# A new order of the steps in the front and in the repeated row of a fused attention and expert kernel

## The chip, the core and the metric

The kernel runs on one core of a Trainium2 chip. A core has a matrix engine (TensorE, PE in the profile; its weight loads are shown as PEld), a vector engine (VectorE, DVE), a scalar engine (ScalarE, ACT), GpSimd (POOL) and SyncE (SP), which here issues the transfers. Each engine works through its own queue of instructions in order and waits on semaphores for the others. The metric is device time in microseconds (us) of one execution, lower is better.

## The reference

Gated linear attention over 4 batches, 8 heads, 768 positions and head size 48, followed by a layer of 8 experts on all 3072 tokens (width 384, hidden 1024), whose weights per token come from a softmax that is balanced by 8 rounds of Sinkhorn scaling.

```python
for t in range(S):
    state = alpha[:, :, t, :, None] * state + np.einsum('bhd,bhe->bhde', k[:, :, t], v[:, :, t])
    y[:, :, t] = np.einsum('bhd,bhde->bhe', q[:, :, t], state)
...
logits = x @ w_gate
P = np.exp(logits - logits.max())
for _ in range(8):
    P /= P.sum(1, keepdims=True) + 1e-09
    P /= P.sum(0, keepdims=True) + 1e-09
    P *= N / E
for e in range(E):
    h = np.maximum(x @ w1[e], 0.0)
    out += P[:, e:e + 1] * (h @ w2[e])
```

## The kernel before

The attention is done in chunks of 128 tokens, 24 in all, two to a unit (12 units of 256 tokens). A chunk turns k, q and the decays so that the head size lies on partitions, forms scores level by level (pairs of 1, 2, 4 ... 64 tokens, each level with the decays multiplied in), multiplies them with v, adds the part of the running state, and writes the result as two half-precision parts (high and low) into `xT`, the input of the experts. Chunks 0 to 3 do all levels directly in 13 steps (`direct_chunk`): step 2 turns the inputs, steps 3 to 9 are the levels, step 10 makes the output in psum (`psy`), step 11 its norm and the new state `ST`, step 12 `xT`, step 13 the gate's logits (`psg`). From chunk 4 on the lower levels come from blocks: a block (`attn_block`, 16 steps for a unit) multiplies q, k and products of them on POOL and DVE and reduces them on DVE (`tmp`, `AB`, `qt`, `al`), and sends the result through memory to the chunk, which then has 6 steps (`attn_chunk`).

The first three experts are computed with the attention still running. Their tiles are generators (`moe_tile`) which give out a "filler" at a time: in a tile's first half nine matmuls into a psum buffer `ps`, a Relu on ACT and the low half `h` on DVE, eight times; in its second half six matmuls of `ps` from `h` and `w2`, evacuated by ACT as `r`. Psum has four buffers for these. A tile is pushed when its tokens' `xT` and the expert's first weight are done. Each expert's weights are loaded, measured and split into two halves in 16 steps (`load_expert`).

What sets the order is one list of words: START up to chunk 7, then UNIT once for every later unit (eight times), with the numbers counted up. A word takes one step of something: `c2` a step of chunk 2, `b3` of block 3, `d2` the decays of a unit, `w1` a step of expert 1's weights, `g` one of the gate's weights, and `f` gives out 0.45 us worth of fillers, by a nominal price of a filler. A capital letter sets `lop` for that step: products that otherwise go to DVE are then put on POOL, or a weight's low half on POOL with an extra pass on ACT. `early_` holds back words whose inputs are not there. On every engine the instructions stand in the order of these words.

When the list is at its end, the rest of the fillers run with the Sinkhorn rounds; then the other five experts follow in a part of their own (`first`, `second`), whose order the list doesn't touch.

Of the kernel before, what the change touches and what calls it, by code (L numbers as in the profile page):

```python
# [25 lines left out]
def tile_gla_moe(ctx: ExitStack, tc: tile.TileContext, q, k, v, alpha, wg, w1, w2, out):  # L26
# [14 lines left out]
    UNIT = 'f f f f f f f f f f f f f f f f c1 f f c0 f B1 f f f f f f f f c1 f f f f f f f f b1 f f B1 f f b1 f f b1 f f b1 f f b1 f B1 f f f f f f c0 f f B2 f f f f f f f f c1 c0 f f B1 f f c1 f c1 f f f f f d1 f f c1 f f f f f f f f f c2 f f f b2 f f f f f f c2 f f f f f f f f f f b2 b2 B2 B2 b2 f c0'.split()
# [718 lines left out]
    w0, w1_, w2_ = (load_expert(e, wAB[e]) for e in range(NA))  # L760
# [84 lines left out]
    def later(a, g):  # L845

        if a[0] not in "bBcd":
            return a
        m = int(a[1:]) + (g * NCH if a[0] == "c" else g)
        return a[0] + str(m) if m < len(chunks if a[0] == "c" else units) else None  # L850


    order = START + [later(a, g) for g in range(NS // NCH, len(units)) for a in UNIT]
    order = [a for a in order if a]
# [308 lines left out]
```

## Time and profile before

| | us |
|---|---|
| median of 3 runs | 1732.25 (1730.5 to 1732.73) |
| profiled execution | 1735.68 |
| its span, first to last instruction | 1734.0 |
| PE busy | 1650.9 |
| DVE, ACT, POOL busy | 1221.1, 796.8, 290.9 |
| mean granted TensorE clock | 0.975 |

A row of the profile names the line, which here is mostly that of a helper (L58, L67, L70), so the tiles tell the steps apart. What stands in brackets in a timeline is the idle time of that engine ahead of the row and what ended it. The attention and the first three experts take the first 840 us or so, the other five experts the rest.

### The profile page before, as it was taken

To read this page: it belongs to the slowest core of one execution; us is meant where nothing else is said; L and a number is where in the kernel's file an instruction comes from. 1 tells how busy PE (TensorE), PEld (TensorE's weight loads), DVE (VectorE), ACT (ScalarE), POOL (GpSimd) and SP (SyncE) were. 2 spreads that over 40 slices of the span, in tenths; PEclk is the share of its full clock that TensorE was granted. 3 is DMA by queue.
4 is the path that set the end of the run, shared out by engine and by line. 5 is a ranking of instruction groups with operands and counts; after the bars stand their busy time and mean duration, and the time that the engine had idled before them with its cause. 6 is when DMAs were issued, how large, how long until landed. Compare 5 with 4: busy or idle time off the path is not lost.

```text
span 1734.0 us, 46403 instructions
## 1 busy us (share of the span) xinstructions
PE 1650.9 (95%) x19984; PEld 1420.5 (82%) x19984; DVE 1221.1 (70%) x2992; ACT 796.8 (46%) x1592; POOL 290.9 (17%) x262
## 2 busy tenths in 40 slices
PE   5679999999999999999999999999999999999999
PEld 4556767777777777776899999999999999999998
DVE  5767767666656766355577878888788867786666
ACT  3456433334333434334465545554555445544443
POOL 2424245435533633000000000000000000000000
PEclk7679999999999999999999999999999999999999
DMA  7153422442243133021202020202020201000001
GB/s 178 37 124 87 105 63 60 100 100 61 59 101 89 48 90 73 24 61 55 69 24 70 29 65 25 69 28 58 28 65 29 51 2 38 2 1 20 29 29 38
DMA packets 149501, 98.91 MB, mean 57 GB/s; under 512 B 108464, under 2 KB 139440, under 8 KB 149296
## 3 DMA queue, kind: packets, MB, share of 16 engines
q1 hardware_dynamic: 149296, 95.95, 21.2%
q8 instruction: 156, 2.56, 0.6%
q14 instruction: 49, 0.40, 0.1%
HBM read 67.63 MB, written 28.30 MB: 55 GB/s over the span
## 4 chain that ended last, share of the span: by engine, by line
PE 78%; DVE 15%; ACT 3%; issue 2%; POOL 1%; DMA 1%; SPq 0%; ACTq 0%; DVEq 0%; POOLq 0%
PE ps L67 49%; PE ps2x L67 12%; PE ps2v L67 3%; PE ps2z L67 3%; DVE h L58 3%; PE ps2y L67 3%; PE psy L67 2%; PE psl L67 2%; DVE hf L58 2%; DVE w L58 1%; ACT h L58 1%; DVE acc L58 1%; DVE decq L58 1%; DVE AB L58 1%; DVE deck L58 1%
## 5 line engine op out<-in xcount | busy, mean ns | idle before, releaser
L67 PE MATMUL ps<-xT,w 128*128 128x256 f16 (+1 forms) x6984 | 806.9, 273 | 16.2 <-DVE h L58 11.5
L67 PEld LDWEIGHTS <-w 128*128 128x128 f16 x6984 | 676.5, 98 | 99.4 <-issue 18.4
L67 PEld LDWEIGHTS <-h 128*128 128x128 f16 x6768 | 588.0, 98 | 118.4 <-issue 9.4
L58 ACT CAST h<-hf 128x896 f16<-128x896 f32 x240 | 224.8, 937 | 337.6 <-DVE hf L58 227.6
L58 DVE TENSOR_TENSOR h<-hf,h 128x896 f16<-128x896 f32 x240 | 261.5, 1089 | 165.5 <-ACT h L58 164.0
L67 PE MATMUL ps<-w,h 128*128 128x384 f16 x1728 | 297.1, 327 | 0.5 <-DVE h L58 0.4
L67 PE MATMUL ps2x<-w,h 128*128 128x192 f16 x2880 | 267.7, 246 | 7.6 <-DVE ps2z L58 5.5
L58 DVE TENSOR_TENSOR hf<-hf 128x128 f32<-128x128 f32 x960 | 235.3, 286 | 39.5 <-ACT hf L58 30.8
L58 DVE SCALAR_TENSOR_TENSOR h<-ps,h 128x256 f16<-128x256 f32 (+1 forms) x296 | 115.6, 411 | 140.9 <-ACT h L58 140.3
L58 ACT ACTIVATE h<-ps 128x256 f16<-128x256 f32 (+1 forms) x296 | 110.3, 377 | 164.1 <-PE ps L67 164.1
L58 ACT ACTIVATE hf<-ps 128x512 f32<-128x512 f32 x240 | 142.4, 593 | 54.1 <-PE ps L67 54.1
L58 POOL TENSOR_TENSOR tmp<-qt,kt 128x768 f32<-128x768 f32 (+1 forms) x80 | 133.2, 1670 | 126.9 <-DVE qt L58 72.7
L58 ACT COPY r<-ps 128x384 f32<-128x384 f32 x72 | 34.4, 479 | 158.5 <-PE ps L67 144.1
L58 DVE TENSOR_REDUCE AB<-tmp 128x16 f32<-128x768 f32 (+2 forms) x90 | 80.7, 903 | 33.5 <-POOL tmp L58 33.3
L67 PE MATMUL ps2v<-w,h 128*128 128x192 f16 x720 | 70.2, 248 | 0.0
L58 ACT COPY A<-psl 16x128 f32<-16x128 f32 (+3 forms) x164 | 52.5, 327 | 37.5 <-PE psl L67 25.3
L67 PE MATMUL ps2y<-w,h 128*128 128x192 f16 x720 | 69.2, 246 | 0.0
L67 PE MATMUL ps2z<-w,h 128*128 128x192 f16 x720 | 69.2, 246 | 0.0
L58 DVE SCALAR_TENSOR_TENSOR acc<-ps2x,pe,acc 128x192 f32<-128x192 f32 x120 | 49.2, 410 | 1.8 <-PE ps2x L67 1.8
L67 PE MATMUL psl<-T 48*32 48x16 f32 (+2 forms) x1472 | 24.1, 219 | 27.4 <-DVE T L58 10.9
L67 PEld LDWEIGHTS psl<-T 48*32 48x32 f32 (+1 forms) x1472 | 20.7, 139 | 31.8 <-DVE T L58 12.4
L58 ACT ACTIVATE w<-w2f,s_w 128x768 f16<-128x768 f32 x35 | 32.6, 933 | 30.5 <-DVE w2f L58 29.1
(186 smaller groups left out, 1325.5 us busy)
## 6 DMA issues: line engine op xcount, KB each, us to landing
raw<-r SPq DMA_DIRECT2D x72, 192.0 KB, 1.9
ri<-raw SPq DMA_DIRECT2D x72, 192.0 KB, 2.4
w1f<-in_moe_w_dram SPq DMA_DIRECT2D x20, 384.0 KB, 7.0
w2f<-in_moe_w_dram SPq DMA_DIRECT2D x5, 1536.0 KB, 7.0
VN<-in_v_dram SPq DMA_DIRECT2D x48, 96.0 KB, 3.0
xT<-in_moe_w_dram SPq DMA_DIRECT2D x6, 768.0 KB, 4.6
out_dram<-acc SPq DMA_DIRECT2D x24, 192.0 KB, 2.0
qt<-in_q_dram SPq DMA_DIRECT2D x10, 384.0 KB, 4.7
```

The source lines that it names most:

```text
L58: r = f(*a, **k_)
L67: tc.keep_in_program_order(nc.tensor.matmul(out_, lhsT, rhs, start=start, stop=stop, **k_))
```

## The change

START and UNIT are replaced by other lists, which were searched for anew with half the TensorE clock assumed at the front. START has 1972 words (1996 before), 1783 of them f (1807); UNIT 131 (132), 102 of them f (103). The other words are the same steps, in other places and with other capitals. The heads of both lists, cut:

```diff
-    START = 'c0 C0 f c0 f c0 c1 f c0 f C1 f f c0 f f f ...'.split()
-    UNIT = 'f f f f f f f f f f f f f f f f c1 f f c0 f B1 f f f f f f f f c1 f f f f f f f f b1 f f B1 f f b1 f f b1 f f b1 f f b1 f B1 f f f f f f c0 f f B2 f f f f f f f f c1 c0 f f B1 f f c1 f c1 f f f f f d1 f f c1 f f f f f f f f f c2 f f f b2 f f f f f f c2 f f f f f f f f f f b2 b2 B2 B2 b2 f c0'.split()
+    START = 'c0 C0 C0 C0 f C1 f c0 f f f f f f f f C1 f f ...'.split()
+    UNIT = 'f f f f f f f f f f f f f f c1 f f c0 f f f f f f f B1 f f f f f b1 f f f f f f f B1 f f f f b1 B1 f f b1 f f B1 b1 f f b1 f f f f f c0 f c1 f f f f f f B2 c1 f f f f f f c0 f f c1 f f f f f d1 f f f f c1 c2 f f f f f f f f c1 f f f f c2 c0 f f f f f f f f b2 f f f f f B2 f b2 f B2 f B2 b2'.split()
```

Where it moves instructions, at three places. First, VectorE at the end of chunk 3 (the names end in batch and chunk, 0_3; `w11` is the low half of expert 1's first weight, `h1_0_256` that of the next tile's h). Before:

```order
L58 TENSOR_TENSOR T_0_3_1249<-T_0_3_1249,D64_0_3_1876 128x2x4x64
L58 SCALAR_TENSOR_TENSOR w11_1_826<-xT0_1_80,s_w1_1_1816,w10_1_825 128x768 x2
L58 TENSOR_SCALAR m_0_3_2010<-psy_0_3_1969 128x128
L58 TENSOR_SCALAR st_0_3_2012<-m_0_3_2010 128x128
L58 TENSOR_TENSOR ys_0_3_2014<-psy_0_3_1969,st_0_3_2012 128x384
L58 TENSOR_SCALAR pw_0_3_2016<-m_0_3_2010 1x128
L58 TENSOR_TENSOR ST0_119<-ST0_119,pss_0_3_2018 48x4x48 x2
L58 SCALAR_TENSOR_TENSOR w11_1_826<-xT1_1_83,s_w1_1_1816,w10_1_825 128x768
L58 TENSOR_TENSOR xT1_0_82<-ys_0_3_2014,xT0_0_79 128x3x128
L58 SCALAR_TENSOR_TENSOR h1_0_256_2036<-ps1_0_256_0_2037,h0_0_256_2035 128x256
```

Now, in the same place:

```order
L58 TENSOR_SCALAR m_0_3_2010<-psy_0_3_1969 128x128
L58 TENSOR_SCALAR st_0_3_2012<-m_0_3_2010 128x128
L58 TENSOR_TENSOR ys_0_3_2014<-psy_0_3_1969,st_0_3_2012 128x384
L58 TENSOR_SCALAR pw_0_3_2016<-m_0_3_2010 1x128
L58 TENSOR_TENSOR ST0_119<-ST0_119,pss_0_3_2018 48x4x48 x2
L58 TENSOR_TENSOR xT1_0_82<-ys_0_3_2014,xT0_0_79 128x3x128
L58 SCALAR_TENSOR_TENSOR w11_1_849<-xT1_1_83,s_w1_1_1740,w10_1_848 128x768
L58 SCALAR_TENSOR_TENSOR h1_0_256_2036<-ps1_0_256_0_2037,h0_0_256_2035 128x256
```

The last split of the weight has moved behind the low half of xT, and the two ahead of chunk 3's norm have left VectorE.

Second, VectorE around block 4's long product (`tmp8_1_1`, of batch 1, unit 1) and the first h's of the tile of tokens 512 to 767 (`h1_0_512`). Before:

```order
L58 TENSOR_REDUCE AB0_123<-tmp4_1_1_22_3378 128x4x4
L58 TENSOR_REDUCE AB0_123<-tmp4_1_1_23_3400 128x4x4
L58 TENSOR_TENSOR qt_1_1_3218<-qt_1_1_3218,al_1_1_3220 128x2x192
L58 TENSOR_TENSOR al_1_1_3220<-al_1_1_3220 128x2x48
L58 TENSOR_TENSOR tmp8_1_1_24_3443<-qt_1_1_3218,kt_1_1_3219 128x1536
L58 SCALAR_TENSOR_TENSOR h1_0_512_3446<-ps1_0_512_0_3447,h0_0_512_3445 128x256
L58 SCALAR_TENSOR_TENSOR h1_0_512_3446<-ps1_0_512_1_3459,h0_0_512_3445 128x256
L58 TENSOR_REDUCE AB0_123<-tmp8_1_1_24_3443 128x4x8
L58 SCALAR_TENSOR_TENSOR h1_0_512_3446<-ps1_0_512_2_3537,h0_0_512_3445 128x256
```

Now:

```order
L58 TENSOR_REDUCE AB0_123<-tmp4_1_1_22_3419 128x4x4
L58 SCALAR_TENSOR_TENSOR h1_0_512_3440<-ps1_0_512_0_3441,h0_0_512_3439 128x256
L58 SCALAR_TENSOR_TENSOR h1_0_512_3440<-ps1_0_512_1_3453,h0_0_512_3439 128x256
L58 TENSOR_REDUCE AB0_123<-tmp4_1_1_23_3428 128x4x4
L58 TENSOR_TENSOR qt_1_1_3181<-qt_1_1_3181,al_1_1_3183 128x2x192
L58 TENSOR_TENSOR al_1_1_3183<-al_1_1_3183 128x2x48
L58 TENSOR_TENSOR tmp8_1_1_24_3469<-qt_1_1_3181,kt_1_1_3182 128x1536
L58 SCALAR_TENSOR_TENSOR h1_0_512_3440<-ps1_0_512_2_3471,h0_0_512_3439 128x256
L58 TENSOR_REDUCE AB0_123<-tmp8_1_1_24_3469 128x4x8
```

Two h's have moved ahead of the block's long step. At the block before it (block 3, tile of expert 1) it is six instead of none.

Third, VectorE in a repeated row, at the end of a block (batch 2, unit 0) and the start of the next tile (`h1_0_1024`). Before:

```order
L58 TENSOR_TENSOR tmp8_2_0_42_5362<-qt_2_0_4712,kt_2_0_4713 128x1536
L58 TENSOR_REDUCE AB0_123<-tmp8_2_0_42_5362 128x4x8
L58 TENSOR_REDUCE AB0_123<-tmp4_2_0_43_5381 128x2x8
L58 TENSOR_REDUCE AB0_123<-tmp4_2_0_44_5396 128x2x8
L58 SCALAR_TENSOR_TENSOR h1_0_1024_5409<-ps1_0_1024_0_5410,h0_0_1024_5408 128x256
L58 TENSOR_TENSOR qt_2_0_4712<-qt_2_0_4712,al_2_0_4714 128x384
L58 TENSOR_TENSOR al_2_0_4714<-al_2_0_4714 128x48
L58 SCALAR_TENSOR_TENSOR h1_0_1024_5409<-ps1_0_1024_1_5425,h0_0_1024_5408 128x256
```

Now:

```order
L58 TENSOR_TENSOR tmp8_2_0_42_5285<-qt_2_0_4653,kt_2_0_4654 128x1536
L58 TENSOR_REDUCE AB0_123<-tmp8_2_0_42_5285 128x4x8
L58 TENSOR_REDUCE AB0_123<-tmp4_2_0_43_5322 128x2x8
L58 TENSOR_REDUCE AB0_123<-tmp4_2_0_44_5331 128x2x8
L58 TENSOR_TENSOR qt_2_0_4653<-qt_2_0_4653,al_2_0_4655 128x384
L58 TENSOR_TENSOR al_2_0_4655<-al_2_0_4655 128x48
L58 SCALAR_TENSOR_TENSOR h1_0_1024_5347<-ps1_0_1024_0_5348,h0_0_1024_5346 128x256
L58 SCALAR_TENSOR_TENSOR h1_0_1024_5347<-ps1_0_1024_1_5380,h0_0_1024_5346 128x256
```

The first h of the next tile has moved behind the block's last two products.

In the front, beside this: chunk 1's first level (step 3) goes ahead of chunk 0's step 8; chunk 3's step 9 ahead of the gate's third; block 2's steps 5 to 8 come earlier (5 and 6 ahead of the first tile, 7 and 8 among its first half), step 9 ahead of chunk 3's step 2; and its loads ahead of chunk 2's on SP's queue. Further on, chunk 7's step 1 comes behind chunk 6's step 5, and the logits of chunk 5 later. At the end the last chunk's logits come eight fillers ahead of the list's end.

More of the change, by code (lines that the diff above doesn't have):

```diff
@@ L41, in tile_gla_moe @@
[L41 removed]
+    START = 'c0 C0 C0 C0 f C1 f c0 f f f f f f f f C1 f f f f f f f f f f f f f f f f f f f f f f f f f C0 f f f f f f f f f f f w0 f f f f f f f f f f f c0 f f f f f f f f f f f f f f f f f f f f f f f f f f f f f f f f f f f f f f f f f f f f f f f f f f f f f f f f f f f f f f f f f f f f f f f f f f f f f f f f f f f f f f f f f f f f f f f f f f B2 f f f f f f f f f f f C1 f f f f f f f f C2 f f f f f f f f f f f f W0 w0 f f f f f f f f c0 c1 f f f f f f f f f w0 f f W0 f f f f f f f f f f f f C2 f f f f f f f f f f f f C1 f f f f w0 f f f f f f f f f f f f f f f f f f f f f f f f f f f f f f c0 f f f w0 f f f f f f f f f f f f f f f f f f C1 f f f f f f f f f f f f w0 f f f f f f f f f f f f f f f f f f f f f f W1 f f f f f f f f f f f f f f f f f f f f f f f f f f f f f f f f f f f f f f f f f f f f f f f f f f f f f f f f f f f C0 f f f f f f f f f f f f f f f f f f f f f f f f f f f f f f f f f f f f f f f f f f f f f f f f f f f f f f f f f f f f f f f f f f f f W1 C1 f f f f f f f f f f f f f f f f f f f f f f f f f f f f f f f f f f f f f f f f f f f f f f f f b2 f f f f f f f f f f f C0 f f f f f f f f f f f f f f f f f f f f f f f f w0 f f f f f f f f f f f f f f f f f f f f f f f f f f f f f f f f f f c1 f f f f f f f f f d2 f f f f f f f f f f f f f f f f f f f f f f f f f f f f f f f f f f f f f f f f f f f f f f f f f f f f f f c2 f f f f f f f B3 f f f f f f f f f f f f f B2 C1 f f f f f f f W0 f C3 f f f f f f f f f f f f f f f f f f f f f f f f f f f C1 f f f f f f f f f f f f f f f f f B2 c1 f f f f f f f f f f f f f f f f f f f f f g f f f f f f f f f f f f f f f f f f B2 f b2 f f c2 f f f f f f f f c0 f f b2 f f b2 f f f f c2 f f f f f f f f f f f f f f f f f c1 f f f w0 f f f f f f f f f f f f f f f f f f f f f f b2 f f f f f f f C3 f f f f f c2 f f f f f f f f f f f f f f f f f f f f f f f f f f f f f f f f W1 C3 f f f f f f f f f f f f f f f f f f f f f f f f f f f f f f f f f f c2 f f c2 f f f f f f f f f f f f f f f f f f f f f f w0 f f f f f f B3 f f f f f f f f f f f f f f f C3 f f f f f f f f f c0 f f f f f f f f f f f f f f c2 f f f f f f f f f f f f f f f f W0 f f f f f f f f f f f W1 f c3 f f f f f f f f w2 f f f f c2 b2 f f f f f f f f f f f f f f f f f f f f f f f f f f f f f f c2 f f f w0 f f f f w0 f f f f f f f f f f f f f f f f f f f f f f f c3 f f b2 f f f f f f g f f f f f f f f f f f f f W0 f f f f f f f f f f f f W1 f f f f C3 f f f f f f f f f f f f f f f f f f f f f f f f f f f f f f f f f f f f f f f f f f f f f f f f f f f f f f f f f f f f f f f f f C2 f f f B2 f f C3 f f f f f f f f b2 f f f f f B3 f w2 f f f f f f f w0 f f f f f w2 f f f f f f f f f f f f b3 f f f f f f f f w2 f f f B3 B2 f f f f f f f f f f f f f f f f f f f f f f f f f f f f f f f f f f f f f f f f f f f f f f f f f f B2 f f f f f f f f f f f f c3 f f C1 f f f g f f f f f f f W1 f d3 f f f f f f f f f f f f f f f f f f W1 f f f f c3 f f f f f f f f f f f f f f c3 f f f f f f f f f C3 w1 f f c4 f f f B3 f f f f W1 f f f f w1 f f f f f f B2 f f f f f f f f f f W1 f f f f f W1 f f f f f f f c4 f w2 f b3 f f f f f f f f f f f f f f f C2 f f w1 f f f f f f f W1 f f f f f f f f f f f f f f f f f f f f f f f f f f f f f f f f f f f f f f f f f f f f f f f f f f f f f f f f f f f f f f f f f f f f f f f f f f f f f f f f f f f f w2 f f f f f f f f f f f w2 f f f f c4 f f f f f f f f f f f f f c4 f w1 f f f f f f f f f f f w2 f f f f f f f f f f f f f f f f f f f f f f f f f f f f f f f f f f f f f f f f f f f f f f f f f f w2 f f f f f c4 f f f f f f f f f f f f f f f f f f w2 f f f f f f f f f w1 f f f f f C3 f f f f f f f f f f f b3 f f f f f f f f f f f f b3 f f f f B3 f f B3 B4 f B3 f f c4 f f c6 f b3 f f f f w2 b3 f f f B3 f f f f f f f f f f f f c5 f f f c5 w2 f f w2 c5 f w2 c5 w2 f f f f f f f f f f f f c5 f f f f w2 f f f f f f b3 f f f b4 f f f f f f f f f f f f f f b4 f w1 b4 f f f f f f f f f f f f c8 B4 f f f f c5 f f B4 f f f b4 f f b4 f f f f f f f f b4 f b4 f B4 c6 f b4 f f f f f B4 f c6 f f B4 f f B4 c6 f f f B4 f f c6 f f f f f c7 c6 f f B5 f c7 f f f f d4 f f f f f f f c7 f f c7 f f f f f f f f f c7 f f c7 c8 b5 B5 f f f f b5 B5 b5 b5 f'.split()
```

1 line of the change is left out of this document (removed).

## The prediction

> **What bounds the kernel now.** I read the page's totals first, then its slices, the busy times by stretch, TensorE's waits, and last the timelines around the longest of them.
>
> ```profile
> PE 1650.9 (95%) x19984; PEld 1420.5 (82%) x19984; DVE 1221.1 (70%) x2992; ACT 796.8 (46%) x1592; POOL 290.9 (17%) x262
> PE   5679999999999999999999999999999999999999
> PEclk7679999999999999999999999999999999999999
> PE 78%; DVE 15%; ACT 3%; issue 2%; POOL 1%; DMA 1%; SPq 0%; ACTq 0%; DVEq 0%; POOLq 0%
> ```
>
> TensorE is the bound: busy 1650.9 of 1734.0 us, and the chain lies on it for 78%. The 83 us in which it stands are mostly in the first three slices of 43 us, where its clock is low too. By stretch (start:end, length, busy time of PE, PEld, DVE, ACT, POOL, granted clock, DMA share, GB/s):
>
> ```profile
> 20.00:45.00 25.00, 12.75 (x478) 10.10 (x478) 11.86 (x33) 10.71 (x25) 2.54 (x5) 0.56 0.75 191
> 65.00:85.00 20.00, 8.62 (x433) 7.55 (x431) 18.13 (x41) 5.11 (x13) 10.65 (x9) 0.73 0.01 3
> sum 127.00, PE 77.74 PEld 62.42 DVE 81.99 ACT 55.42 POOL 41.38; mean PE 12.96 PEld 10.40 DVE 13.66 ACT 9.24 POOL 6.90
> sum 194.00, PE 181.54 PEld 137.11 DVE 137.56 ACT 90.29 POOL 80.58; mean PE 36.31 PEld 27.42 DVE 27.51 ACT 18.06 POOL 16.12
> 320.00:740.00 420.00, 415.84 (x5386) 318.09 (x5385) 260.14 (x502) 158.81 (x428) 168.94 (x129) 1.00 0.29 71
> 740.00:845.00 105.00, 97.75 (x750) 73.90 (x748) 57.60 (x156) 42.24 (x87) 0.00 (x0) 0.98 0.27 72
> ```
>
> The first sum is 0 to 127 us, the direct chunks 0 to 3: 49 us without TensorE. The second is 126 to 320: 12.5 us. The repeated row (320 to 740) loses 4.2 us, the change of phase behind it 7.2, and the order there is untouched. So the edit can win in a front where no engine is full and chunks go back and forth between PE and DVE, and in single waits up to 320; in the repeated row it can mostly lose.
>
> **The change part by part.** Every step is still taken once. Only places move, and by a step's capital letter some multiplications go from DVE to POOL or back. An "f" ahead of the first pushed tile emits nothing, so the f's at START's head are no time. TensorE's work and SP's transfers are the same in sum.
>
> *End of chunk 3.* The next tile's matmuls wait for chunk 3's low half of xT.
>
> ```profile
> 124.00 0.72 DVE L58 TENSOR_TENSOR ST<-ST,pss 48x192 f32<-48x192 f32 x2
> 124.76 1.02 DVE L58 SCALAR_TENSOR_TENSOR w<-xT,s_w,w 128x768 f16<-128x768 f32 x1
> 125.69 0.55 DVE L58 TENSOR_TENSOR xT<-ys,xT 128x384 f16<-128x384 f32 x1
> 126.30 4.00 PE L67 MATMUL ps<-xT,w 128*128 128x256 f16 x18 [1.48 <-DVE xT L58]
> ```
>
> A weight split of 1.02 us stands between ST and xT; it now stands behind xT: -1.0 (between -1.5, all of the wait, and 0). The two splits of that weight ahead of it go to POOL, with two passes on ACT instead of one; that is beside chunk 3's psy, so 0.
>
> *Gate weights.* Chunk 3's last level (16 small matmuls) moves ahead of the gate's.
>
> ```profile
> 112.41 0.84 ACT L58 COPY A<-psl 32x128 f32<-32x128 f32 x4
> 113.64 0.62 PE L67 MATMUL psg<-wg,xT 128*128 128x8 f16 x9 [2.60 <-ACT wg L58]
> 116.41 1.12 PE L67 MATMUL psl<-T 48*64 48x64 f32 x16
> 118.55 1.51 PE L67 MATMUL psy<-T,ST 128*32 128x128 f32 x24 [1.01 <-DVE T L58]
> ```
>
> The level still waits for ACT's copies out of psl (to 113.25), so most of the 2.60 stays; but DVE's T behind it then lies beside the gate's matmuls, and the 1.01 goes: -1.0 (-2.6 to 0).
>
> *First levels of chunks 0 and 1, first tile.* Chunk 1's scores now go ahead of chunk 0's sixth step, into TensorE's waits of 1.20 and 0.37.
>
> ```profile
> 23.36 0.60 PE L67 MATMUL psl<-T 48*32 48x32 f32 x28 [1.20 <-DVE A L58]
> 25.07 1.02 PE L67 MATMUL psl<-T 48*32 48x16 f32 x64 [0.37 <-DVE A L58]
> 29.78 0.43 PE L67 MATMUL psl<-T 48*32 48x16 f32 x28 [2.17 <-issue]
> 37.72 0.69 PE L67 MATMUL psl<-T 48*32 48x16 f32 x46 [3.81 <-issue]
> 30.00:35.00 5.00, 3.01 (x127) 2.55 (x113) 3.40 (x15) 1.56 (x4) 0.62 (x1) 0.50 1.06 243
> ```
>
> Behind them TensorE stands 2.17 and 3.81 us for nothing but its own issue, while the DMA engines are full (1.06). The same weights are loaded by then (b2's q, alpha and k only go ahead of chunk 2's loads on SP's queue, which chunk 2 first needs at 42 us), so whoever comes earlier waits longer: I take 0 of the 1.57. The Trainium skill's page "Runtime: NRT & Kernel Launch" (Instruction fetch mechanics) has the cost of crossing a block of code as mostly hidden; by it the 1.57 would be kept. This trace disagrees, if these stalls are the code's.
>
> Then b2's steps come sooner: two of them go in among the first tile's eight h's, and chunk 3's first T goes behind the long DVE step of b2.
>
> ```profile
> 72.06 0.69 DVE L58 TENSOR_TENSOR T<-psQR,D 128x512 f32<-128x512 f32 x1 [0.16 <-ACT QR L58]
> 78.07 0.94 DVE L58 TENSOR_REDUCE AB<-tmp 128x16 f32<-128x768 f32 x1
> 81.36 0.55 DVE L58 TENSOR_TENSOR xT<-ys,xT 128x384 f16<-128x384 f32 x1
> 82.86 0.84 PE L67 MATMUL psl<-T 48*32 48x16 f32 x64 [3.78 <-DVE T L58]
> ```
>
> The long step takes 78.07 to 81.4 and TensorE stands 3.78 us behind it now. In the new order chunk 3's T stands behind it: it would come at about 78.9 instead of 72.06, some 6.8 us later, while the b2 work is over sooner. DVE has the same rows ahead of the second tile either way (the sum of their mean durations is 82.8 us in both orders). I take 0, with -1.6 and +6.8 as ends. Front: -2.0.
>
> *From 126 to 275 us.* Four waits lose their cause.
>
> ```profile
> 181.68 2.13 PE L67 MATMUL ps<-xT,w 128*128 128x256 f16 x18 [1.80 <-DVE h L58]
> 204.68 0.20 PE L67 MATMUL psg<-wg,xT 128*128 128x8 f16 x2 [1.07 <-ACT xT L58]
> 205.45 0.33 PE L67 MATMUL psg<-wg,xT 128*128 128x8 f16 x7 [0.56 <-DVE xT L58]
> 240.29 2.13 PE L67 MATMUL ps<-xT,w 128*128 128x256 f16 x18 [1.70 <-DVE h L58]
> 246.82 0.66 PE L70 MATMUL psq<-ident,QN 128*128 128x128 f32 x4 [0.68 <-ACT Tk L58]
> 174.65 1.75 DVE L58 TENSOR_TENSOR tmp<-qt,kt 128x1536 f32<-128x1536 f32 x1
> 236.53 3.37 DVE L58 TENSOR_TENSOR tmp<-qt,kt 128x1536 f32<-128x1536 f32 x1
> ```
>
> The 1.80 and 1.70 have one cause: a block's long product (tmp, 1.75 to 3.37 us) stands on DVE ahead of the tile's first h's, and TensorE runs out of psum buffers. In the new order six h's stand ahead of it in the first place, and two in the second. From the first I take -1.3, as the last two h's still wait (0 to -1.8); from the second -1.7 (0 to -1.9). Of the psg waits 1.63 go, since fillers lie between xT and psg now, but chunk 5's psy and its norm follow each other without a filler, for about the 0.6 us from ACT's ab: -1.0 (-1.6 to +0.6). Chunk 7's transposes come after chunk 6 has given its psum buffer back: -0.7. Sum -4.7.
>
> *Repeated row.* Each row has had a wait of about 0.5 us for DVE's decq:
>
> ```profile
> PE psl L67 <- DVE decq L58: 2.5, 5, 0.5
> 307.14 3.11 PE L67 MATMUL ps<-xT,w 128*128 128x256 f16 x27 [1.39 <-DVE h L58]
> 753.53 0.27 PE L70 MATMUL pst_gg<-ident,gm 128*1 128x128 f32 x1 [0.96 <-DVE gm L58]
> ```
>
> Five fillers lie now between a chunk's transposes and its scores instead of four: at most -2.5; I take -1.0. At the end the last logits come eight fillers before the phase ends, so gm is ready when TensorE gets to it: -1.0 (-1.3 to +1).
>
> *Waits that the new order makes.* The old trace can't show them. The sum so far removes 8.7 us of waits that I could see; an order with the same work must have some of its own (126 to 320 has 12.5 us now, of which I listed 5.8). I give 40% back, +3.5; ends 0 and +11.
>
> Sum: -2.0 - 4.7 - 1.0 - 1.0 + 3.5 = -5.2. The profiled execution took 1735.68 us (span 1734.0 and 1.7 around it), so 1730.5; the median shown, 1732.25, is 3.4 below that execution, which gives 1727.1.
>
> **The rivals.**
>
> *Nothing is given back.* Without the +3.5 it is 1723.6, and with the 1.57 us of the first levels 1722.0. For it: the placed waits each have one cause that is gone. Against it: the 3.81 us of issue.
>
> *No change.* The 6.8 us of chunk 3's T decide the front: its six levels follow one another, each a PE block of about 0.85 and a T of 0.69. Then -5.2 + 6.8 = +1.6, 1733.9. For it: the wait of 3.78 us shows such a chain. Against it: from 65 to 85 us DVE is busy 18.13 of 20, so what b2 no longer needs later comes back.
>
> *Slower, by the repeated row.* In the new row a block's last reduces, qt and al all stand on DVE ahead of the first h of the next tile; before, that h stood ahead of qt and al. The 1.39 us above at 307 is such a wait, in the one place where the old order had it so. If every one of the eight rows has it, it is 8 x 1.39 = 11.1 on top of the other terms without the row's -1.0: +6.9, 1739.2. It turns slower by over 0.2% (3.5 us) from 1.0 us per row, (3.5 + 4.2) / 8. Against it: seven or eight second-half fillers of about 0.96 us, which need nothing of DVE, now lie over the block's rows.
>
> *A better clock in the front.* Between 20 and 45 us TensorE's 12.75 us run at a granted clock of 0.56. If shorter gaps kept the clock full there, they would take 12.75 x 0.56 = 7.1; with half of the 5.6 us saved on the path, since DVE is about as busy, it is 2.8 less: 1724.3. For it: waits of 1.20 and 0.37 are filled. Against it: the 2.17 and 3.81 stay. The Trainium skill's "TensorE: Matmul & The Clock Gate" (Part 1) speaks for it: an idle window of about 3.4 us halves the clock and a busy one restores it; here the low clock outlasts windows in which TensorE was busy half the time, so the trace neither bears it out nor excludes it.
>
> **How the numbers follow.** A run of this kernel differs from no change visibly at about 0.2%, 3.5 us. Forecast, 1727.1 (1724.5 to 1728.7): 0.44. Nothing given back, 1722 to 1724: 0.10. A better clock, 1724: 0.04. No change, 1728.8 to 1735.7: 0.25. Slower: 0.17. So faster 0.58, same 0.25, slower 0.17. The range leaves about 2 in 10 out: its low end is 2 below the rival without new waits, its high end lies short of the full repeated row. The forecast's own range is 1723 to 1730.
>
> **What would show it.** Right: the w split behind chunk 3's xT and the first 256-wide matmul at about 124 instead of 126.3; no wait over 1 us for h near 180 and 240, none for psg near 205; TensorE busy over 183 us between 126 and 320; gm's wait gone. The issue stalls near 28 and 34 stay and end at about the same times. Wrong: chunk 3's xT after 127; a wait of 1 us or more for h in each repeated row; or new waits between 126 and 275 of more than 5 us in all.

## The result, and the profile after

| | before | after |
|---|---|---|
| median, us | 1732.25 (1730.5 to 1734.55) | 1721.51 (1719.51 to 1725.42) |
| ratio | 1 | 0.9939 (95%: 0.9927 to 0.995) |
| profiled execution, its span, us | 1735.68, 1734.0 | 1721.51, 1719.8 |
| PE, DVE, POOL busy, us | 1650.9, 1221.1, 290.9 | 1645.5, 1203.7, 283.4 |

Faster by 10.7 us (8.7 to 12.6). The forecast was 5.2 us faster, 1727.1, with a range of 1720 to 1737 that takes in the rivals: the sign and that range held, the size is twice what was said, and the forecast's own range, 1723 to 1730, was missed by 1.5 us. The page of the changed kernel, its totals and the clock row of its slices:

```profile
PE 1645.5 (96%) x19984; PEld 1419.6 (83%) x19984; DVE 1203.7 (70%) x2993; ACT 793.1 (46%) x1592; POOL 283.4 (16%) x261
...
PEclk9789999999999999999999999999999999999999
```

Two things changed: TensorE stands less (74.3 us instead of 83.0), and it is busy 5.4 us less with the same matmuls. Both are found by stretch. First of before, then of the changed kernel; the stretches end at 130 us, at 262 us, at the largest logit (gm) and at the end; the columns are length, PE busy, granted clock, DMA share, GB/s.

```profile
0.00:130.00 130.00, 80.74 (x2308) 0.73 0.47 113
130.00:262.00 132.00, 121.65 (x1479) 0.98 0.34 86
262.00:753.50 491.50, 484.60 (x6303) 1.00 0.29 71
753.50:1734.00 980.50, 963.96 (x9899) 1.00 0.13 39
```

```profile
0.00:130.00 130.00, 87.36 (x2350) 0.87 0.50 120
130.00:262.00 132.00, 123.95 (x1569) 1.00 0.36 90
262.00:738.80 476.80, 469.88 (x6148) 1.00 0.30 73
738.80:1719.80 981.00, 964.31 (x9923) 1.00 0.13 37
```

The two spans differ by 14.2 us, the medians by 10.7: the execution of before that was profiled is 3.4 us above its median, so its front is not to be taken as typical (see "All of them in one account"). Idle time is length less busy time. It falls by 6.6 us in the front (49.3 to 42.6) and 2.3 in the next stretch (10.3 to 8.0). In the repeated row it is 6.9 in both, at the end 16.5 and 16.7. The rest is clock. In before the clock behind 130 us is at half to 132.2 us, and then for single periods of 3.41 us, beginning at 166.4, 511.1, 801.3 and 845.6 us; in the changed kernel there is none. Two of the four, each with the period ahead of it, in before (busy times of PE, PEld, DVE, ACT, POOL, then the clock):

```profile
507.70:511.10 3.40, 1.74 (x84) 1.38 (x84) 2.74 (x6) 0.77 (x2) 1.06 (x1) 1.00 0.00 0
511.10:514.50 3.40, 3.40 (x67) 2.69 (x57) 0.95 (x2) 1.66 (x5) 1.60 (x1) 0.50 0.02 5
797.80:801.30 3.50, 0.83 (x8) 0.75 (x8) 0.76 (x2) 3.44 (x9) 0.00 (x0) 0.99 0.00 0
801.30:804.70 3.40, 3.40 (x18) 2.42 (x17) 1.51 (x4) 1.92 (x6) 0.00 (x0) 0.51 0.00 0
```

Ahead of each of the four stands a period in which TensorE stood for about half of the time or more (busy shares 0.47, 0.51, 0.23 and 0.42). TensorE is busy all through the halved one, and loses half of it, 1.7 us: the 256-column matmuls in the period at 801.3 us start 0.213 us apart, those at full clock 0.109. The waits ahead of it are ordinary ones (TensorE's timeline; in brackets the wait):

```profile
509.43 1.14 PE L67 MATMUL ps<-xT,w 128*128 128x256 f16 x9 [1.66 <-DVE h L58]
...
800.47 4.77 PE L67 MATMUL ps<-xT,w 128*128 128x256 f16 x27 [2.76 <-DVE h L58]
```

In the changed kernel the wait of 2.76 has become two, 1.46 and 1.39 us, and an edge of a period (787.7) falls between them:

```profile
784.30:787.70 3.40, 1.94 (x17) 1.49 (x16) 0.00 (x0) 3.33 (x8) 0.00 (x0) 1.00 0.08 29
787.70:791.10 3.40, 2.01 (x19) 1.75 (x18) 1.77 (x5) 2.15 (x7) 0.00 (x0) 1.00 0.10 34
791.10:794.50 3.40, 3.40 (x30) 2.69 (x29) 1.94 (x9) 1.85 (x4) 0.00 (x0) 1.00 0.00 0
```

Nearly the same idle time, parted by an edge, leaves the clock alone here. Over the fourteen profiles of this study, behind 130 us, each of the 21 periods in which TensorE was busy for a share of 0.43 or less was followed by one at half clock, none with 0.62 or more was. In between both occur: of 17 periods from 0.43 to 0.52 six were followed by one at half clock, of 52 from 0.52 to 0.62 two were. "Clock loss" below is half of TensorE's busy time in such periods: 7.8 us behind 130 us in before, 0 in the changed kernel.

### The profile page after: what moved, and what is told of

Its sections match the earlier page's. It is cut to its first block, busy times and chain, and to the rows that moved or that the text cites. A ratio compares the mean times of both kernels' runs of the same rounds, so it can differ in the third digit from the quotient of the medians.

```text
span 1719.8 us, 46369 instructions
## 1 busy us (share of the span) xinstructions
PE 1645.5 (96%) x19984; PEld 1419.6 (83%) x19984; DVE 1203.7 (70%) x2993; ACT 793.1 (46%) x1592; POOL 283.4 (16%) x261
## 4 chain that ended last, share of the span: by engine, by line
PE 74%; DVE 17%; ACT 4%; issue 2%; POOL 2%; DMA 1%; ACTq 0%; SPq 0%; POOLq 0%; DVEq 0%
PE ps L67 46%; PE ps2x L67 12%; DVE h L58 4%; PE ps2z L67 3%; PE ps2v L67 3%; PE ps2y L67 3%; DVE hf L58 2%; PE psy L67 2%; DVE AB L58 2%; PE psl L67 2%; POOL tmp L58 2%; DVE tmp L58 2%; ACT h L58 2%; DVE w L58 2%; ACT w L58 1%
## 5 line engine op out<-in xcount | busy, mean ns | idle before, releaser
L67 PE MATMUL ps<-xT,w 128*128 128x256 f16 (+1 forms) x6984 | 806.9, 273 | 10.3 <-DVE h L58 4.0
L67 PEld LDWEIGHTS <-w 128*128 128x128 f16 x6984 | 676.0, 98 | 90.8 <-issue 12.6
L67 PE MATMUL ps<-w,h 128*128 128x384 f16 x1728 | 293.4, 326 | 3.7 <-DVE w L58 1.9
L58 POOL TENSOR_TENSOR tmp<-qt,kt 128x768 f32<-128x768 f32 (+1 forms) x80 | 125.2, 1569 | 161.0 <-DVE AB L58 86.9
L58 ACT COPY r<-ps 128x384 f32<-128x384 f32 x72 | 34.3, 478 | 195.4 <-PE ps L67 150.9
L58 ACT COPY A<-psl 16x128 f32<-16x128 f32 (+3 forms) x164 | 52.5, 327 | 36.5 <-PE psl L67 26.8
L58 DVE SCALAR_TENSOR_TENSOR acc<-ps2x,pe,acc 128x192 f32<-128x192 f32 x120 | 49.3, 411 | 1.8 <-PE ps2x L67 1.8
L58 ACT ACTIVATE w<-w2f,s_w 128x768 f16<-128x768 f32 x35 | 32.4, 933 | 27.3 <-DVE w2f L58 27.3
```

Of the source, the lines that this page charges most:

```text
L58: r = f(*a, **k_)
L67: tc.keep_in_program_order(nc.tensor.matmul(out_, lhsT, rhs, start=start, stop=stop, **k_))
```

## The experiments

The expectations speak of a theory of the clock at first (the new head keeps the clock full from 23 us on, and that is the gain), then of a theory of the grid (the periods of 3.41 us, as above, behind 130 us). The theory of the waits is the forecast's own. In the diffs f11 stands for eleven words f. Each ratio is to before, with its 95% interval.

### The new front alone (e1_front)

```diff
-    order = START(new) + UNIT(new) x 8
+    order = START(new) up to chunk 3's step 12 + all steps left over in the order of before
```

> The changed kernel's steps up to chunk 3's transposed input (xT), then the steps of the kernel before in their old order (the steps it had already done ahead of that point left out). Theory of the clock and of the fetch stall (the new head fills TensorE's throttle period up to 23.0 us, the granted clock stays full to about 60 us, and chunk 3's xT comes 4.5 us earlier, all of which is kept): about 1727.8 us against 1732.25, ratio 0.9974, and no period at half clock begins at 23.0 us. Theory of the waits (the front is worth what the forecast gave it, the weight split and the gate weights, 2.0 us): 1730.2 us, ratio 0.9988. Third possibility (what is early at chunk 3 only waits later, since the old middle is bound by VectorE): 1732, ratio 1.000.

Measured 1730.62 us, ratio 0.9992 (0.9984 to 1.0001): -1.5 us. Nothing like the 4.5 us by which chunk 3's xT comes earlier in the traces is kept. The value is near the forecast's front (-2.0), and 0 is inside its interval; that it is the front's waits is not shown, since this profile also has fewer periods at half clock further on than before (two, 3.2 us). The half clock began at 23.0 us here as in before.

### The new order to chunk 7, the old row (e2_rowold)

```diff
-    UNIT = (new)
+    UNIT = (before)
```

> The changed kernel's order up to chunk 7 with the repeated row of before. Theory from the two traces (the lead is made ahead of 310 us, about 9.8 us, and the new row is worth about nothing but the 0.96 us wait for the largest logit at the end, its new waits taking back what the removed ones gave): 1722 to 1723 us, ratio 0.9945 to 0.995 against before. Theory of the forecast (the new row gains 2.0 for waits removed and loses 3.5 in new ones): 1720.0 us, ratio 0.993. Third possibility (the row is worth the 3 to 4 us by which the lead grows between 310 us and the end): 1724.5 to 1726, ratio 0.9955 to 0.9965.

Measured 1728.45 us, 0.9978 (0.9968 to 0.9988): -3.7 us, beyond the slow end of all three. All three were wrong: the row is worth some 6.9 us once the new front is there, though TensorE's idle time in it is the same in before and in the changed kernel. The profile of this mixture shows what it pays: 10.4 us idle in the row (a wait of 4.2 us for the decays' transfer is one), and three periods at half clock, two behind that wait, one at 834.7 us.

### Is it the clock in the front? (e3_swapback, e5_fill)

In the changed kernel, and the other way round in before:

```diff
-    START = '... B2 f11 C1 f8 C2 f12 W0 w0 f8 c0 c1 ...'
+    START = '... B2 f11 c0 C1 f8 C2 f12 W0 w0 f8 c1 ...'
```

```diff
-    START = '... W0 f16 C2 f7 c0 W0 f25 W0 f3 c1 f9 ...'
+    START = '... W0 f16 C2 f7 c1 c0 W0 f25 W0 f3 f9 ...'
```

> The changed kernel with one step moved: chunk 0's eighth step goes back ahead of chunk 1's third step (its scores), as it stood before. Theory of the clock: TensorE is again under half busy in the throttle period that ends at 23.0 us, a long period at half clock begins there, and the kernel loses 3 to 4.5 us: 1724.5 to 1726 us, ratio to before 0.9955 to 0.9965. Theory of the waits: no wait that the forecast counted comes back, at most the 1 to 2 us of work that no longer fills a stall: 1721.5 to 1723 us, ratio 0.994 to 0.995, whatever the clock shows.

> The kernel before with the one step moved the other way: chunk 1's third step (its scores) ahead of chunk 0's eighth step. Theory of the clock: the period up to 23.0 us is filled, the granted clock stays full to about 60 us, 3 to 4.5 us are gained: 1727.8 to 1729.3 us, ratio 0.9974 to 0.9983. Theory of the waits: 1731 to 1732.3 us, ratio 0.9993 to 1.000. Rival to both: what keeps TensorE idle there is not the order of these two steps but the fetch stalls, and the half clock begins at 23.0 us as before: ratio 1.000.

Measured 1721.74 (0.9942, 0.993 to 0.9953) and 1732.46 (0.9997, 0.9989 to 1.0006): the swap is worth nothing either way. The theory of the clock in the front falls, and not because the clock stayed low. The profile of before with the swap has the full clock up to 72 us, and the kernel gains nothing by it:

```profile
0.00:130.00 130.00, 82.76 (x2318) 0.87 0.49 118
```

The full clock there is not the swap's doing either. Two kernels of the next section, f1_before20 and f2_before31, have before's order in the front without the swap. Between 12 and 72 us one has a mean clock of 0.63, the other the full clock (the two rows below, in this order), and both start the matmuls behind the wait for chunk 3's xT at the same time, 124.18 and 124.25 us:

```profile
12.00:72.00 60.00, 39.63 (x1302) 33.11 (x1301) 35.65 (x88) 28.11 (x66) 17.50 (x21) 0.63 0.48 123
12.00:72.00 60.00, 38.59 (x1300) 31.88 (x1300) 34.81 (x86) 28.04 (x66) 16.27 (x20) 1.00 0.50 123
```

The unchanged kernel says the same. Over the 59 timed executions of before that ran beside all these experiments the mean granted clock lay between 0.974 and 0.988 (in the profiles the difference lies in the front); the spans average 1730.4 us in the 24 where it was below 0.98 and 1731.1 in the 35 above. The clock of the first 130 us differs from one execution to the next, and no cost of it shows.

### Does the place of the periods count? (f1_before20, f2_before31, f3_after23, f4_after31)

If the periods' places decide, then added work that pushes later waits over an edge must cost less, or more, than itself. In the first half of the tile of expert 2 at token 768, ahead of the first matmul of piece 4:

```diff
+    for _ in range(20 if (e, t0, f, n) == (2, 768, 4, 0) else 0):
+        mm(ps[:, :T], w1h[i][:, c, f * P:(f + 1) * P], xs(j, c, t0, T), start=True, stop=True)
     mm(ps[:, :T], w1h[i][:, c, f * P:(f + 1) * P], xs(j, c, t0, T), start=(n == 0), ...)
```

> The kernel before, with 20 matmuls of 256 columns repeated near 350 us (each is overwritten by the next, so they compute nothing; 20 x 0.109 us = 2.18 us of TensorE). Theory of the grid (the clock is granted in periods of 3.413 us that stand at the same places of the program in every profile; a period in which TensorE is idle for more than about half makes the next one run at half clock, which costs 1.71 us where TensorE is the bound): the waits at 507.8 and 797.7 us are moved over the edge of a period (1.19 and 0.47 us on its two sides, 1.38 and 1.38 us) and no longer halve the clock at 511 and 801 us, that at 843.3 us still does: 2.18 - 2 x 1.71 = -1.2 us, about 1731.0 us, ratio 0.9993. Theory of the waits alone: the added work is paid in full, +2.2 us, 1734.4, ratio 1.0013. Third: TensorE is not the bound there, ratio 1.000.

> The same with 31 repeated matmuls, 31 x 0.109 = 3.38 us, which is one period. Theory of the grid: all waits stand to the edges as before, the same three periods are at half clock, +3.4 us, 1735.5 us, ratio 1.0020, so 1.2 us more work than with 20 repeats costs 4.6 us more. Theory of the waits alone: +3.4 us, and 1.2 us above the kernel with 20 repeats. Third: ratio 1.000.

> The changed kernel with 23 matmuls repeated near 340 us, 23 x 0.109 = 2.51 us. Theory of the grid: the waits at 785.2 and 787.8 us (1.46 and 1.39), which an edge parts in the changed kernel, come into one period (2.27 us of idle time), and so do the two at 830.3 and 832.0 us (2.13 us): two periods at half clock appear near 791 and 835 us, 2.51 + 2 x 1.71 = +5.9 us, about 1727.5 us, ratio to before 0.9973. Theory of the waits alone: +2.5 us, 1724.1, ratio 0.9953.

> The changed kernel with 31 matmuls repeated, 3.38 us, one period. Theory of the grid: no period at half clock after 130 us, as in the changed kernel, +3.4 us, 1725.0 us, ratio 0.9958: less than with 23 repeats, though there is 0.9 us more work. Theory of the waits alone: also +3.4 us, but 0.9 us more than with 23 repeats.

On the changed kernel: 1726.68 us with 2.51 us of work added (0.9968, 0.9955 to 0.998) and 1723.69 with 3.38 added (0.9949, 0.9937 to 0.9962). The medians are 5.2 and 2.2 us above the changed kernel's, so the larger addition is the cheaper, as the theory of the grid had it and the theory of the waits did not, though the two intervals overlap by a little. The profiles show the mechanism: with 23 repeats both waits near 786 us fall into one period; with 31, one period's length, they stay parted.

```profile
786.60:790.00 3.40, 1.14 (x9) 0.87 (x9) 0.00 (x0) 3.34 (x10) 0.00 (x0) 1.00 0.16 58
790.00:793.40 3.40, 2.62 (x13) 1.83 (x13) 1.51 (x5) 1.47 (x5) 0.00 (x0) 0.51 0.00 0
```

```profile
788.30:791.70 3.40, 1.73 (x17) 1.40 (x15) 0.00 (x0) 3.19 (x8) 0.00 (x0) 1.00 0.04 14
791.70:795.10 3.40, 2.01 (x19) 1.65 (x18) 1.63 (x5) 2.29 (x7) 0.00 (x0) 1.00 0.12 45
795.10:798.50 3.40, 3.40 (x31) 2.73 (x29) 2.08 (x9) 1.70 (x4) 0.00 (x0) 1.00 0.00 0
```

The second pair near 830 us was expected in one period too, and wasn't (the edges stood 0.4 us off). So the profile with 23 repeats has 1.3 us of clock loss, which is less than the medians' difference; and the two executions that were profiled, 1724.6 and 1725.65 us, stand the other way round. The medians carry the result, and its size is not accounted for.

On before it failed: 1736.19 (1.0023, 1.0014 to 1.0032) and 1738.99 us (1.0032, 1.0019 to 1.0045), +3.6 where -1.2 was expected, and +6.4 where +3.4 was. The second addition costs 2.8 us more than the first, where the grid gave 4.6 and the waits 1.2. The execution with 20 repeats that was profiled had come to its row 1.0 us earlier against the periods than the profile of before, so 3.3 us of a wait at 797 us, itself 3.65 now, lay in one period again; the wait of 1.66 us at 508 lay in one as well and halved nothing this time. That the periods stand at the same places of the program in every execution is therefore not so. Ten profiles share the order up to chunk 7 with before or with the changed kernel (but for the swap). At their 3000th matmul, near 190 us, the periods stood at the same place to 0.1 us in six of them; in the other four they were 0.2 to 1.0 us off.

### The new row alone (h_rownew), the weight split alone (e4_split)

```diff
-    UNIT = (before)
+    UNIT = (new)
```

```diff
-    START = '... c3 f8 w1 f7 C3 f9 W1 ...'
+    START = '... c3 f8 f7 C3 w1 f9 W1 ...'
```

> The order of before up to chunk 7 with the new repeated row, the counterpart of the kernel with the new order up to chunk 7 and the old row. If the two parts add: 1732.3 - 6.9 = 1725.4 us, ratio 0.996. Theory of the grid: what the new row saves is not waits (TensorE's idle time between 262 us and the largest logit is 6.9 us in both) but the periods at half clock at 511, 801 and 845 us, which depend on where the waits stand to the edges of the periods; with the old front the row starts 11.4 us later, which is 1.2 us more than three periods, and the waits at the end then just miss the two bad places: no such period, 3 x 1.71 = 5.1 us gained, 1727.2 us, ratio 0.997. Theory of the waits alone: the row is worth 0 to 1 us, 1732, ratio 0.9995.

> The kernel before with one step moved: the second expert's eighth weight step (the split on VectorE that its input for chunk 3 waited behind, 1.48 us at 124.3 us) goes behind chunk 3's twelfth step. Forecast's term: -1.0 us (-1.5 to 0), 1731.3, ratio 0.9994. Theory of the grid: -1.5 us or less idle time, and the positions of all later waits move by it; which of the four periods at half clock (166, 511, 801, 845 us) stay can change the time by 1.7 us each: 1725 to 1732 us.

The new row behind the old front: 1741.76 us, 1.0056 (1.0043 to 1.0068), 9.3 us slower than before. None of the theories had that. With -3.7 for the new order to chunk 7 alone (e2_rowold) and -10.7 for both, the parts don't add: by themselves they give +5.6. TensorE's largest group of waits in this mixture between 275 and 800 us (total, times, longest; in before the same group has 3.0 us):

```profile
PE ps L67 <- DVE h L58: 11.4, 6, 2.4
```

One of the four of 2.4 us, TensorE and VectorE in the mixture (first fence), and the same VectorE product in the changed kernel (second):

```profile
410.77 3.36 DVE L58 TENSOR_TENSOR tmp<-qt,kt 128x1536 f32<-128x1536 f32 x1
414.06 0.41 DVE L58 SCALAR_TENSOR_TENSOR h<-ps,h 128x256 f16<-128x256 f32 x1
...
414.53 0.82 PE L67 MATMUL ps<-w,h 128*128 128x384 f16 x2 [2.39 <-DVE h L58]
```

```profile
345.24 5.20 PE L67 MATMUL ps<-w,h 128*128 128x384 f16 x31
...
346.99 3.36 DVE L58 TENSOR_TENSOR tmp<-qt,kt 128x1536 f32<-128x1536 f32 x1
...
350.28 1.47 PE L67 MATMUL ps<-xT,w 128*128 128x256 f16 x12
```

The block's long product takes VectorE 3.36 us in both. In the changed kernel TensorE works through second-half pieces then (5.2 us of `ps<-w,h`, which need nothing of VectorE). In the mixture the last low half `h` of a tile stands behind the product, and the next matmuls need it. The word f only says "a piece of whatever tile is next": which piece meets the product is settled by how many pieces the front has given out. So a row is good or bad for a given front, not by itself.

The split alone (some transfers on SP's queue between 133 and 144 us change their order with it): 1732.59 us, 0.9997 (0.9988 to 1.0006). The forecast's -1.0 lies inside, so does 0. In its profile the wait at 124 us is 0.55 instead of 1.48, and the idle time between 130 and 262 is 11.9 us instead of 10.3: more than what was won at 124 us is idle again.

### A better row (g_f2, g_f2pad)

```diff
-    UNIT = '... B2 c1 f f f f f f c0 ...'
+    UNIT = '... B2 f f c1 f f f f c0 ...'
```

> The changed kernel with the second chunk's third step (which reads the decayed queries Tq) two filler words later in the row: one expert piece of TensorE work (0.96 us) more stands ahead of it in each of the repeated rows. Theory of the waits: the waits for Tq (5.1 us in seven rows) go but for 0.7 us, -4.4 us, 1717.1 us, ratio to before 0.9912. Theory of the grid: all that follows comes 4.4 us (one period and 1.0 us) earlier, the waits near 785 and 830 us fall into one period each, two periods at half clock appear there and take 3.4 us back: -1.0 us, 1720.5 us, ratio 0.993. Third: other work of the row falls behind and the waits only change their names: 1721.5.

> The same with 14 repeated matmuls near 340 us (14 x 0.109 = 1.53 us of added work, overwritten). Theory of the waits: 1.5 us slower than without them, 1718.6 us, ratio 0.9921. Theory of the grid: 2.9 us earlier instead of 4.4, the waits near 785 and 830 us stay parted by edges, no period at half clock: -2.9 us, 1718.6 us, ratio 0.992, 1.9 us faster than without the added work.

1719.01 us (0.9923, 0.991 to 0.9937) and 1719.31 us (0.9924, 0.9911 to 0.9936): both beat the changed kernel's median, by 2.5 and 2.2. The waits for Tq are gone (5.1 us in the changed kernel, none here; the idle time in the row falls from 6.9 to 2.6). Without added work a period at half clock comes back, the gain is 2.5 instead of 4.3; with 1.53 us of work added there is none, and the time is the same. The halved period, without added work:

```profile
781.90:785.40 3.50, 1.14 (x9) 0.87 (x9) 0.04 (x1) 3.44 (x10) 0.00 (x0) 0.99 0.16 56
785.40:788.80 3.40, 2.96 (x15) 2.10 (x15) 1.80 (x5) 1.14 (x4) 0.00 (x0) 0.50 0.02 5
```

The added work was paid for, but the 1.9 us in its favour that the theory of the grid gave did not come, since only one of two expected periods had been halved.

### All of them in one account

Idle time and clock loss of the profiled execution behind 130 us, with the added work; their sum against that of before (33.7 + 7.8 = 41.5); beside it what the timed medians say, each against the runs of before beside it (us).

| kernel | idle | clock loss | added | sum | measured |
|---|---|---|---|---|---|
| e5_fill | 33.8 | 6.8 | | -0.9 | +0.3 |
| e4_split | 35.2 | 6.8 | | +0.5 | +0.2 |
| e1_front | 35.4 | 3.2 | | -2.9 | -1.5 |
| e2_rowold | 33.9 | 4.3 | | -3.3 | -3.7 |
| changed kernel | 31.6 | 0 | | -9.9 | -10.7 |
| e3_swapback | 31.6 | 0 | | -9.9 | -10.4 |
| h_rownew | 41.9 | 6.7 | | +7.1 | +9.3 |
| g_f2 | 27.3 | 1.5 | | -12.7 | -13.4 |
| g_f2pad | 27.3 | 0 | 1.5 | -12.7 | -13.1 |
| f1_before20 | 36.5 | 3.4 | 2.2 | +0.6 | +3.6 |
| f2_before31 | 35.5 | 6.9 | 3.4 | +4.3 | +6.4 |
| f3_after23 | 32.2 | 1.3 | 2.5 | -5.5 | -5.9 |
| f4_after31 | 31.9 | 0 | 3.4 | -6.2 | -8.9 |

The sum is within 1.4 us in nine of thirteen and within 3.0 in all. Without the clock loss the changed kernel would be given -2.1 instead of -9.9. It does without the front: the idle time up to 130 us lies between 42.3 and 49.3 us over these profiles, 43.2 to 49.3 (mean 46.6) with the old order there and 42.3 to 46.7 (mean 44.4) with the new, so about 2 us less, within what one execution differs from the next.

The front is the open end of this account. The first matmuls behind the wait for chunk 3's xT start at 117.7 to 123.0 us (mean 121.1) in the eight profiles with the new order there, at 124.2, 124.3 and 123.6 in f1_before20, f2_before31 and h_rownew, which share before's order up to chunk 7, and at 126.3 in the profile of before, the latest of all. By that the new front is worth some 3 us, and the sum of the changed kernel would be about -13. The account is also measured against one execution of before, which is 3.4 us above its median. The good agreement is thus in part luck. That TensorE loses time in the halved periods is shown; how the 10.7 us divide between clock and front is known to some 3 us only.

## Why the prediction was right in sign, and where its size went wrong

The sign was forecast for a cause that is there: waits of the old order went away. That the time lies in the wide range although most of the gain behind 130 us has another cause is luck.

*Front, -2.0.* The end of chunk 3 came as said: the split stands behind xT, and the wait of 1.48 us is 0.55, nearly the -1.0. VectorE's and TensorE's timelines of the changed kernel, there and at the places of the other terms of the front:

```profile
121.20 0.56 DVE L58 TENSOR_TENSOR xT<-ys,xT 128x384 f16<-128x384 f32 x1
121.81 1.02 DVE L58 SCALAR_TENSOR_TENSOR w<-xT,s_w,w 128x768 f16<-128x768 f32 x1
...
121.82 2.50 PE L67 MATMUL ps<-xT,w 128*128 128x256 f16 x12 [0.55 <-DVE xT L58]
...
28.69 0.43 PE L67 MATMUL psl<-T 48*32 48x16 f32 x28 [3.03 <-issue]
...
34.71 0.69 PE L67 MATMUL psl<-T 48*32 48x16 f32 x46 [2.02 <-issue]
...
108.77 1.27 PE L67 MATMUL psl<-T 48*64 48x64 f32 x16 [2.41 <-ACT A L58]
...
111.24 0.63 PE L67 MATMUL psg<-wg,xT 128*128 128x8 f16 x9 [0.69 <-ACT wg L58]
```

The matmuls behind the wait were expected at 124 and start at 121.8. The two issue stalls, which were to end at the same times, end 1.1 and 3.0 us sooner than in the profile of before. That is not the new order's doing: with before's order up to chunk 7 they end at 27.3, 28.0 and 27.1 and at 35.0, 35.7 and 34.3 us in f1_before20, f2_before31 and h_rownew, where the profile of before has 29.8 and 37.7 and the changed kernel 28.7 and 34.7. So the 0 for the first levels stands, and the step that fills their waits is worth nothing in time (e3_swapback, e5_fill). The Trainium skill's "mostly hidden" cost of crossing a block of code, in "Runtime: NRT & Kernel Launch" (Instruction fetch mechanics), is still contradicted by the stalls, 3.03 and 2.02 us here, if they are the code's; what they are no run here tells. The gate weights gave 0.5 instead of 1.0: waits of 2.60, 1.01, 0.32 and 0.30 became 2.41, 0.69, 0.37 and 0.21. Chunk 3's first T comes at 75.75 instead of 72.06, 3.7 us later and not 6.8, and the long wait of that chunk, 3.78 us before and 3.97 now, ends at 77.6 instead of 82.9 (79.4 to 80.9 in the three profiles named above). So what the no-change rival feared did not come.

*126 to 275 us, -4.7.* The named waits went nearly as sized: h 1.80 to 0.54 and 1.70 to 0.60, psg from 1.63 to 0.24, psq's 0.68 gone, -4.4. The 0.6 for ACT's ab, which the forecast had set against the psg waits, came too, 0.60 at 196.4 us: -3.8 against -4.7.

```profile
178.20 4.72 PE L67 MATMUL ps<-w,h 128*128 128x384 f16 x28 [0.54 <-DVE h L58]
...
232.07 1.14 PE L67 MATMUL ps<-xT,w 128*128 128x256 f16 x9 [0.60 <-DVE h L58]
...
242.54 0.37 PE L67 MATMUL psg<-wg,xT 128*128 128x8 f16 x9 [0.24 <-ACT Tk L58]
```

```profile
126.00:320.00 194.00, 184.53 (x2469) 140.90 (x2467) 137.92 (x272) 92.43 (x239) 85.65 (x66) 1.00 0.36 90
```

TensorE is busy 184.5 us between 126 and 320, above the 183 named. The idle time between 130 and 262 fell by 2.3 only, so about 1.5 came back as new waits, of the kind that the +3.5 stood for.

*Repeated row, -2.0, and the rest of the +3.5.* The waits for decq and gm are gone, as said; new ones for Tq took their place:

```profile
PE psy L67 <- DVE Tq L58: 5.1, 7, 1.6
```

Together 0 in idle time up to the largest logit. In waits alone, then, the forecast's order of size was right behind the front: -2.3 + 0 against -4.7 - 2.0 + 3.5 = -3.2.

*The term that failed is one that the sum didn't have.* Clock loss behind 130 us was put at 0 without a reason; it was 7.8 us in the profiled execution of before and 0 in that of the changed kernel. The row that shows it, 0.98 as the clock between 740 and 845 us, was quoted and not read: 105 us at 0.98 is about 2 us. The rival that spoke of the clock put it in the front, where it is low and no cost of it shows (e5_fill, f1_before20 against f2_before31). It counts where TensorE is full.

*The other rivals.* "Nothing is given back", 1722.0 to 1723.6, came nearest in time by a wrong road: waits were given back. "Slower, by the repeated row" did not happen in the changed kernel, but its mechanism, h behind the block's VectorE work in each row, is most of what made the new row behind the old front 9.3 us slower (waits for h 11.4 us instead of 3.0). It was weighed by the row alone, and hangs on front and row together.

## What to carry to other kernels

Where TensorE is full, price a wait by more than its length. Idle time that filled 57% or more of one period of 3.41 us cost up to 1.7 us more in the next every time here, and up to 38% of it never did. Splitting such a wait, or moving it over an edge, can give that back; but the edges stood elsewhere in four executions of ten, so a place found in one profile does not hold in the next, and taking the wait away, as g_f2 did, is the surer gain. Read the granted clock where TensorE is full and not where it is lowest. And value an order of steps as a whole: halves of two good orders made one that is worse than either, since which work covers a long instruction is set by all that was handed out before.

## What the runs showed of the hardware

The halving of the clock by single waits was not expected. A wait of 1.66 us, with TensorE busy for 1.74 of 3.40 us, was followed by a period at half clock at 511 us in before and at the same place in e5_fill and f2_before31, and was not in f1_before20. Two shorter waits in one period, 1.33 and 0.79 us, did it at 845.6 us in before. The Trainium skill's "TensorE: Matmul & The Clock Gate" (Part 1) has a window of 3413 ns, free-running; the length agrees with the periods here. Its advice in "Why this matters for your kernels" is to avoid idle gaps of more than about 3 us between bursts of matmuls; the waits named here are shorter. One period in which TensorE was busy for a share of 0.78 or more brought the full clock back each time behind 130 us; the only one with less, 0.54 at 667.5 us in e2_rowold, did not. That executions of one front met the periods at the same places to 0.1 us in six of ten cases was not expected of a free-running window either; why, no run here tells.
